# Two blocks of wo per layer, loaded as five columns by sixteen DMA engines and a sixth by six

## The chip, the core and the metric

The kernel runs on one core of one Trainium2 chip. The metric is the device time of one execution in microseconds (us), the median over runs; lower is better. "The profile" is a record of one execution by the hardware profiler, "the trace" the events behind it. Engines: PE does matmuls (PEld its weight loads), DVE and ACT work on vectors, POOL sets constants, SP issues every load; sixteen DMA engines carry the bytes from HBM to SBUF.

## What is computed

One token passes two layers, each an attention over the last 4096 cached keys (32 heads of 192) and a mixer:

```python
q = (x @ wq) in 32 heads of 192
scores = einsum(q, k) * Dh**-0.5          # k, v: the last 4096 of 32768 rows of the caches
o = einsum(softmax(scores), v)            # 32 x 192, as one row of 6144
A(x) = o @ wo                             # wo: 6144 x 640
x = x + A(layernorm(x));  x = x + B(layernorm(x), w1, w2, w3, w4)
x = x + A(layernorm(x));  x = x + B(layernorm(x), w1, w2, w3, w4)
```

With one token every shift in B moves its row out of range, so B is x plus a gelu between w3 and w4. Both layers use the same weights and caches, and nearly all of them are read twice: 216.47 MB from HBM.

## The kernel before

**Groups.** The 32 heads are worked in 8 groups of 4 (QH), backwards in layer 0 and forwards in layer 1. For a head, DVE transposes its keys in 32x32 blocks (line 377), PE forms scores (453), the group's softmax follows (lines 476 to 538), PE multiplies the probabilities with the values (569), and o_fold (578) leaves the group's output in oT: 128 partitions by 6 columns, partition 32 h + r holding elements 6 r to 6 r + 5 of head h. A group's projection by wo waits in `pending` until the next group's first scores are under way.

**Projection.** wo's 768 rows of one group lie in a cell as 128 partitions by 6 columns of 640: partition p holds the rows 6 p to 6 p + 5. In the groups of `rows` (line 726) out_row (608) takes oT's columns one by one as weights and streams wo's columns past them, in two halves of 320, into rows 0 and 32 of a PSUM tile; add (619) adds both rows into `acc` on DVE, and turn_row (629) turns the sum into a column at the end. The other groups use out_proj (591).

**Loads.** All loads are issued on SP in the order of layer_stream (205): wq and x, then K and V loads by turns, with one wo after the four V of a group. A K or V head is 128 partitions of 12288 bytes, 1.5 MB; a wo block 128 of 7680 bytes. They go into 11 cells of SBUF that are taken and given back in turn. The order of each engine's instructions is written out by hand in attention (641); the framework adds the waits. It gives the loads eight completion counters in turn, so that a load also waits until the load eight before it, which used the same counter, has completed.

**Others that the change touches.** `ones` (264), a 128x128 matrix of ones, is the weight of every sum over partitions (lines 325, 338, 528, 681, 866, 868). At the start PE runs 66 small matmuls (WARM, lines 77 and 310) while it waits for loads. row_space (352) gives the room for acc.

Of the kernel before, what the change touches and what calls it, by code (L numbers as in the profile page):

```python
# [8 lines left out]
BF16 = mybir.dt.bfloat16  # L9
F32 = mybir.dt.float32  # L10
# [7 lines left out]
P = 128  # L18
# [17 lines left out]
def kernel(  # L36
# [14 lines left out]
    nc = tc.nc  # L51
    _, _, D = A_x.shape
    _, H, Sk, Dh = A_k_cache.shape
# [20 lines left out]
    NA = Dh // 32  # L74
    NKX = 6
    NKEEP, NCELL = 7, 11
    WARM = 66

# [6 lines left out]
    assert W4C % 2 == 1 and W4C < NF  # L85
    GROUPS = [[list(range(h, h + QH)) for h in range(0, H, QH)] for _ in range(2)]
    GROUPS[0].reverse()

    head = ctx.enter_context(tc.tile_pool(name="head", bufs=1))
    fixed = ctx.enter_context(tc.tile_pool(name="fixed", bufs=1))  # L90
# [66 lines left out]
    def load_wq(layer, kc):  # L157
        nc.sync.dma_start(wq_sb[:, kc, :], A_wq[kc * P:(kc + 1) * P, :])
        return wq_sb

    def load_wo(layer, c):
        t = take(("wo", layer, c))
        src = A_wo[c * QC:(c + 1) * QC, :].rearrange("(p c) n -> p (c n)", c=NA)
        parts = {NG - 2: (3, 3), NG - 1: (3, 2, 1)}.get(c, (NA,)) if layer == 1 else (NA,)
        i = 0
        for n in parts:
            nc.sync.dma_start(t[:, i * D:(i + n) * D], src[:, i * D:(i + n) * D])
            i += n
        return t
# [121 lines left out]

    Lq = const.tile([P, 32], F32, name="Lq")
    nc.vector.reduce_sum(Lq[:], ident[:].rearrange("p (j a) -> p a j", j=4), axis=AX.X)
    eps1 = head.tile([P, 1], F32, name="eps1")
    nc.vector.memset(eps1[:], eps)

# [25 lines left out]
    def ln_center(x, rowsum):  # L322

        mean_ps = psm.tile([P, 1], F32, tag="psm")
        nc.tensor.matmul(mean_ps[:], lhsT=ones[:], rhs=rowsum[:, 0:1], start=True, stop=True)
        xc = big.tile([P, ND], BF16, name="xc")
        nc.vector.scalar_tensor_tensor(out=xc[:], in0=mean_ps[:, 0:1].broadcast_to([P, ND]), scalar=-1.0 / D,
                                       in1=x[:], op0=ALU.mult, op1=ALU.add)
        xcf = big.tile([P, ND], F32, name="xcf")
        nc.vector.scalar_tensor_tensor(out=xcf[:], in0=mean_ps[:, 0:1].broadcast_to([P, ND]), scalar=-1.0 / D,  # L330
                                       in1=x[:], op0=ALU.mult, op1=ALU.add)
        junk = sm.tile([P, ND], F32, tag="ln_junk")
        ssq = sm.tile([P, 1], F32, tag="ln_ssq")
        nc.scalar.activation(junk[:], xcf[:], ACTF.Square, accum_out=ssq[:, 0:1])

        def total():
            var_ps = psm.tile([P, 1], F32, tag="psm")
            nc.tensor.matmul(var_ps[:], lhsT=ones[:], rhs=ssq[:, 0:1], start=True, stop=True)
            return var_ps

        return xc, xcf, total
# [131 lines left out]
    def softmax_steps(n, ST_ps, sc):  # L473
# [25 lines left out]
        def spread_max():  # L499
            nb_ps = psm.tile([P, 1], F32, tag="psm")  # L500
            nc.tensor.matmul(nb_ps[:], lhsT=held["w"],  # L501
                             rhs=ones[0:1, 0:1], start=True, stop=True)
# [14 lines left out]
        def swap():  # L517
            ng = NGK // NT
            PT_ps = psm.tile([P, n, NJ4, NGK], F32, tag="psm")
            src = held["PrT"].rearrange("p (g j i) -> p i j g", g=ng, j=NJ4)  # L520
            for m in range(NM):
                for q in range(NT):
                    nc.tensor.matmul(PT_ps[32 * m:32 * (m + 1), :, :, ng * q:ng * (q + 1)], lhsT=Eq[:, q, :],  # L523
                                     rhs=src[:, m:QW:NM], start=True, stop=True)
            PT = big.tile([P, n, NJ4 * NGK], BF16, name="PT")
            nc.scalar.copy(PT[:].rearrange("p h c -> p (h c)"), PT_ps[:].rearrange("p h j g -> p (h j g)"))  # L526
            l_ps = psm.tile([P, QH], F32, tag="psm")
            nc.tensor.matmul(l_ps[:], lhsT=ones[:], rhs=held["lh"][:], start=True, stop=True)  # L528
            held["lps"] = l_ps
            return PT  # L530

# [73 lines left out]
                give(("wo", layer, c))  # L605
        return y_ps

    def out_row(layer, c, oT, acc, first):

        wo_t = need("wo", layer, c)  # L610
        N = D // 2
        yr_ps = psm.tile([33, N], F32, tag="psm")
        for k in range(NA):
            for i in range(2):
                nc.tensor.matmul(yr_ps[32 * i:32 * i + 1, :], lhsT=oT[:, k:k + 1],  # L615
                                 rhs=wo_t[:, k * D + i * N:k * D + (i + 1) * N], start=(k == 0), stop=(k == NA - 1))
        give(("wo", layer, c))

        def add():
            for i in range(2):  # L620
                r = slice(32 * i, 32 * i + 1)
                if first:
                    nc.vector.tensor_copy(acc[r, :], yr_ps[r, :])
                else:
                    nc.vector.tensor_add(acc[r, :], acc[r, :], yr_ps[r, :])

        return add

    def turn_row(acc):
        y_ps = psm.tile([P, ND], F32, tag="psm")  # L630
        N = D // 2
        for n in range(ND):
            a, b = n * P, (n + 1) * P
            for i in range(2):
                lo_, hi = max(a, i * N), min(b, (i + 1) * N)
                if lo_ < hi:
                    nc.tensor.matmul(y_ps[lo_ - a:hi - a, n:n + 1], lhsT=acc[:, lo_ - i * N:hi - i * N],  # L637
                                     rhs=ident[0:33, 32 * i:32 * i + 1], start=True, stop=True)
        return y_ps

    def attention(layer, x_cur, rs_cur, x_new, z_new, rs_new, ss_new):
# [29 lines left out]
        def add_y(y_ps, n):  # L671
            y_new = x_new if n == 0 else sm.tile([P, ND], F32, name="y_acc")
            if n == 1:

                rs = big.tile([P, 1], F32, name="rs_y")
                nc.vector.scalar_tensor_tensor(out=y_new[:], in0=y_ps[:], scalar=1.0, in1=y[0][:],
                                               op0=ALU.mult, op1=ALU.add, accum_out=rs[:, 0:1])

                def center():
                    nm_ps = psm.tile([P, 1], F32, tag="psm")  # L680
                    nc.tensor.matmul(nm_ps[:], lhsT=ones[:], rhs=rs[:, 0:1], start=True, stop=True)
# [12 lines left out]
            y[0] = y_new  # L694
# [39 lines left out]
        for gi, cur in enumerate(groups):  # L734
            nxt = list(enumerate(groups[gi + 1])) if gi + 1 < len(groups) else []
            ST_n = None
            if nxt:
# [24 lines left out]
                else:  # L762
# [5 lines left out]
                    part_max()  # L768
                    T(h0, 1)
                    S(h0, 0, ST_n, 0)  # L770
                    turn_max()
                    full_max()
                    S(h0, 1, ST_n, 0)
# [6 lines left out]
                        q[0]()  # L780
                    in_row = gi - 1 in rows
                    if pending is not None:
                        y_ps = out_row(layer, *pending, acc, gi - 1 == rows[0]) if in_row else out_proj(layer, pending)
                    turn_p()
                    T(h1, 0)
                    if q:
# [73 lines left out]
    def mixer(layer, x_cur, z, rs_cur, ss_cur, x_new, rs_new):  # L860
# [2 lines left out]


        s1_ps = psm.tile([P, 1], F32, tag="psm")
        nc.tensor.matmul(s1_ps[:], lhsT=ones[:], rhs=rs_cur[:, 0:1], start=True, stop=True)
        s2_ps = psm.tile([P, 1], F32, tag="psm")
        nc.tensor.matmul(s2_ps[:], lhsT=ones[:], rhs=ss_cur[:, 0:1], start=True, stop=True)
# [119 lines left out]
```

## Time and profile before

| | |
|---|---|
| median of 3 runs | 519.93 us (519.73 to 520.03) |
| the profiled execution | 519.84 us |
| its span, first to last instruction | 518.0 us |
| busy: PE, PE weight loads, DVE, ACT | 324.8, 192.6, 295.2, 49.5 us |
| instructions | 9589, of them PE 4146 matmuls and 4146 weight loads |
| moved by DMA | 217.08 MB, 419 GB/s on average |
| mean granted PE clock | 0.700 |

How to read the lines below: a row of "busy tenths" or GB/s cuts the span into 40 equal slices. A window's row gives start and end, its length, the busy time of PE, PEld, DVE, ACT and POOL with the number of instructions, PE's granted clock, the share of the sixteen DMA engines that was busy (packets overlap a little, so it can pass 1) and GB/s. A timeline row gives start, duration, engine, line, operation and tile; SPq is SP's queue of loads. A row of one tile gives the shortest, median and longest duration in ns, the first and the last start in us and the shapes.

### The profile page before, as it was taken

How to read it: one execution, taken by the hardware profiler on the slowest of the kernel's cores; microseconds unless marked ns; L12 is line 12 of the kernel's file. 1: busy time of each engine (PE TensorE's matmuls, PEld its weight loads, DVE VectorE, ACT ScalarE, POOL GpSimd, SP SyncE). 2: the span in 40 equal slices, each digit the busy share in tenths (PEclk: the TensorE clock that was granted, in tenths of full speed). 3: DMA queues.
4: the chain of work that ended last, by engine and by line, in shares of the span. 5: the costliest groups of instructions: out<-in, count | busy, mean ns of one | idle time of the engine just before them, and what ended most of it. 6: DMA issues, size and time to landing. Idle time of an engine off the chain costs nothing.

```text
span 518.0 us, 9589 instructions
## 1 busy us (share of the span) xinstructions
PE 324.8 (63%) x4146; PEld 192.6 (37%) x4146; DVE 295.2 (57%) x589; ACT 49.5 (10%) x175; POOL 4.0 (1%) x16
## 2 busy tenths in 40 slices
PE   2057656666664566767755866777566856648665
PEld 2024334333332334434333634434333433425334
DVE  2067667575584655656624356567675765664722
ACT  1000101010010100001011111001010101001011
POOL 2000000000000000000000000000000000000000
PEclk9999878565586755677665778557785676776855
DMA  8999999999999999999999999999999999999995
GB/s 347 433 425 426 433 426 427 432 428 425 433 426 427 431 426 429 428 426 431 424 425 396 385 426 429 428 428 428 429 426 427 432 428 426 426 434 426 427 416 235
DMA packets 23949, 217.08 MB, mean 419 GB/s; under 512 B 2532, under 2 KB 3044, under 8 KB 8420
## 3 DMA queue, kind: packets, MB, share of 16 engines
q1 hardware_dynamic: 23908, 216.48, 99.0%
q8 instruction: 32, 0.52, 0.4%
q14 instruction: 9, 0.07, 0.0%
HBM read 216.47 MB, written 0.00 MB: 418 GB/s over the span
## 4 chain that ended last, share of the span: by engine, by line
DMA 50%; PE 23%; DVE 22%; issue 2%; ACT 1%; SPq 1%; DVEq 0%; ACTq 0%
DMA cell<-in_A_k_cache_dram 39%; DVE cell L377 16%; DMA cell<-in_A_v_cache_dram 9%; PE ST_ps L453 9%; PE O_ps L569 7%; DVE o_sb L576 2%; DMA cell<-in_B_w_dram 2%; DVE pm L478 1%; PE nb_ps L501 1%; DVE o_sb L512 1%; ACT o_sb L507 1%; PE y_ps L637 1%; PE l_ps L528 1%; PE PT_ps L523 1%; PE qT_ps L407 1%
## 5 line engine op out<-in xcount | busy, mean ns | idle before, releaser
L453 PE MATMUL ST_ps<-cell,Qblk 128*16 128x256 bf16 x1536 | 163.7, 380 | 106.9 <-DVE cell L377 69.4
L377 DVE STREAM_TRANSPOSE cell<-cell 128x768 uint32<-128x768 uint32 x228 | 204.1, 945 | 15.2 <-DMA cell<-in_A_k_cache_dram 14.9
L453 PEld LDWEIGHTS <-Qblk 128*16 128x16 bf16 x1536 | 86.1, 111 | 176.5 <-issue 150.3
L569 PE MATMUL O_ps<-cell,PT 128*2 128x384 bf16 x1018 | 99.9, 461 | 8.2 <-DMA cell<-in_A_v_cache_dram 7.4
L576 DVE STREAM_TRANSPOSE o_sb<-O_ps 128x384 f32<-128x384 f32 x64 | 37.2, 581 | 111.8 <-PE O_ps L569 111.6
L569 PEld LDWEIGHTS <-PT 128*2 128x2 bf16 x1024 | 46.0, 100 | 22.1 <-issue 10.1
L512 DVE STREAM_TRANSPOSE o_sb<-o_sb 128x256 bf16<-128x256 bf16 x16 | 7.1, 446 | 33.2 <-ACT o_sb L507 24.2
L584 ACT ACTIVATE oT<-oT_ps,rl 32x6 bf16<-32x6 f32 x40 | 10.3, 258 | 164.0 <-PE oT_ps L583 157.8
L583 PEld LDWEIGHTS oT_ps<-o_sb,Lq 128*32 128x32 f32 x160 | 13.3, 145 | 19.3 <-issue 15.8
L583 PE MATMUL oT_ps<-o_sb,Lq 128*32 128x6 f32 x160 | 13.9, 195 | 10.4 <-DVE o_sb L576 9.9
L589 ACT ACTIVATE oT<-oT_ps,rl 32x6 bf16<-32x6 f32 x24 | 6.2, 258 | 107.6 <-PE ST_ps L453 87.1
L407 PE MATMUL qT_ps<-xc,wq_sb 128*128 128x1 bf16 x210 | 7.1, 165 | 12.8 <-DMA wq_sb<-in_A_wq_dram 12.0
L523 PE MATMUL PT_ps<-o_sb,Eq 128*32 128x32 bf16 x256 | 7.3, 237 | 9.3 <-DVE o_sb L512 4.1
L523 PEld LDWEIGHTS <-Eq 128*32 128x32 bf16 x256 | 5.4, 108 | 19.8 <-issue 19.7
L421 DVE TENSOR_TENSOR Xq<-qT_ps,maskq 128x24 bf16<-128x24 f32 (+1 forms) x18 | 2.8, 158 | 17.1 <-PE qT_ps L407 17.1
L396 PE MATMUL qr_ps<-wq_sb,xc 128*1 128x384 bf16 x90 | 12.1, 415 | 0.0
L407 PEld LDWEIGHTS <-wq_sb 128*128 128x128 bf16 x210 | 6.7, 102 | 14.0 <-DMA wq_sb<-in_A_wq_dram 13.0
L504 ACT COPY nb_sb<-nb_ps 128x1 f32<-128x1 f32 x16 | 2.5, 159 | 94.6 <-PE nb_ps L501 94.6
L615 PE MATMUL yr_ps<-cell,oT 128*1 128x320 bf16 x108 | 11.2, 355 | 0.0
L528 PE MATMUL l_ps<-lh,ones 128*128 128x4 f32 x32 | 7.7, 310 | 4.9 <-ACT PT L526 4.9
L428 PE MATMUL Qrep_ps<-Xq,Lb 128*128 128x24 bf16 (+1 forms) x18 | 3.2, 178 | 11.1 <-DVE Xq L421 10.8
L588 PE MATMUL oT_ps<-o,Lq 128*32 128x6 f32 x48 | 6.1, 199 | 6.5 <-DVE o L587 6.5
(143 smaller groups left out, 200.9 us busy)
## 6 DMA issues: line engine op xcount, KB each, us to landing
cell<-in_A_k_cache_dram SPq DMA_DIRECT2D x57, 1536.0 KB, 26.3
cell<-in_A_v_cache_dram SPq DMA_DIRECT2D x57, 1536.0 KB, 25.8
cell<-in_A_wo_dram SPq DMA_DIRECT2D x13, 960.0 KB, 26.5
wq_sb<-in_A_wq_dram SPq DMA_DIRECT2D x5, 1536.0 KB, 12.2
cell<-in_A_v_cache_dram SPq DMA_DIRECT2D x4, 768.0 KB, 23.8
cell<-in_A_v_cache_dram SPq DMA_DIRECT2D x2, 1248.0 KB, 11.5
cell<-in_B_w_dram SPq DMA_DIRECT2D x1, 1536.0 KB, 11.9
cell<-in_B_w_dram SPq DMA_DIRECT2D x2, 768.0 KB, 10.3
```

The source lines that it names most:

```text
L377: nc.vector.transpose(Tu, Ku[:, :, q * NY:(q + 1) * NY])
L396: nc.tensor.matmul(qr_ps[32 * i:32 * i + 1, :], lhsT=xc[:, kc:kc + 1], rhs=wq_sb[:, kc, t0 * P + i * N:t0 * P + (i + 1) * N], start=(kc == ...
L407: nc.tensor.matmul(qT_ps[:, tl:tl + 1], lhsT=wq_sb[:, kc, t * P:(t + 1) * P], rhs=xc[:, kc:kc + 1], start=(kc == 0), stop=(kc == ND - 1))
L453: nc.tensor.matmul(ST_ps[r:r + QW, :].rearrange("p (g i) -> p g i", g=ng), lhsT=Q[:, n, :], rhs=T4[:, :, f, :, t], start=(hq == 0 and n == ...
L512: nc.vector.transpose(held["PrT"], held["Pr"])
L523: nc.tensor.matmul(PT_ps[32 * m:32 * (m + 1), :, :, ng * q:ng * (q + 1)], lhsT=Eq[:, q, :], rhs=src[:, m:QW:NM], start=True, stop=True)
L528: nc.tensor.matmul(l_ps[:], lhsT=ones[:], rhs=held["lh"][:], start=True, stop=True)
L569: nc.tensor.matmul(O_ps[r:r + 2, :], lhsT=PT[:, hq, 2 * i:2 * i + 2], rhs=v_pair(V, h, 2 * i * Dh, 2 * Dh), start=(i < 4), stop=(i >= NB - 4))
L576: nc.vector.transpose(o_sb[:], O_ps.rearrange("p (e a c) -> p e c a", e=2, c=NA))
L583: nc.tensor.matmul(oT_ps[r, :], lhsT=Lq[:], rhs=o_sb[:, e, :, e], start=(e == 0), stop=(e == 1))
L584: nc.scalar.activation(oT[r, :], oT_ps[r, :], ACTF.Copy, scale=rl[r, 0:1])
L615: nc.tensor.matmul(yr_ps[32 * i:32 * i + 1, :], lhsT=oT[:, k:k + 1], rhs=wo_t[:, k * D + i * N:k * D + (i + 1) * N], start=(k == 0), stop= ...
```

## The change

Two of the eight wo blocks of each layer (the groups 2 and 3 in the order of work, counted from 0) are loaded in seven loads in place of one. Columns 0 to 4 of all 128 partitions come in one load, packets of 6400 bytes. The sixth column's 128 pieces of 640 elements come in six small loads with packets of 1280 bytes, to 56 partitions and three places behind the five columns. The first four take 24 pieces each, and their source is ordered with an outermost size of six; the fifth takes 24 from three blocks of eight; the sixth takes 8.

So that the pieces meet the right elements of oT, spread_low multiplies oT's sixth column by three constant selections (Sel) into a tile of 64 by 3, which ACT copies to oX. out_row then makes, for these groups, 5 x 2 matmuls with oT and 6 x 2 with oX in place of 6 x 2, into four PSUM rows in place of two, and add works on four rows. acc grows from 33 to 97 partitions, and turn_row's constant (E2) sums the rows in pairs.

`ones` becomes one column, read 128 times by its address pattern. WARM falls from 66 to 14.

```diff
-    WARM = 66
+    WARM = 14
...
+    SPLIT = [{GROUPS[layer][g][0] // QH for g in gs} for layer, gs in enumerate(((2, 3), (2, 3)))]
+    NE, NU, LOW = 6, NA - 1, 24
...
+    def load_wo_split(t, src):
+
+        def low(at, col, rows):
+            nc.sync.dma_start(t[at:at + LOW, col * D:(col + 1) * D],
+                              src[rows:rows + LOW, NU * D:].rearrange("(b a) n -> a b n", a=NE))
+
+        nc.sync.dma_start(t[:, 0:NU * D], src[:, 0:NU * D])
+        for h in range(QH):
+            low(32 * (h % 2), NU + h // 2, 32 * h)
+        rest = src[:, NU * D:].rearrange("(h r) n -> h r n", r=32)[:, LOW:, :]
+        e = slice((NU + 2) * D, (NU + 3) * D)
+        nc.sync.dma_start(t[0:LOW, e], rest[0:QH - 1])
+        nc.sync.dma_start(t[32:64 - LOW, e], rest[QH - 1])
...
     def load_wo(layer, c):
         t = take(("wo", layer, c))
         src = A_wo[c * QC:(c + 1) * QC, :].rearrange("(p c) n -> p (c n)", c=NA)
+        if c in SPLIT[layer]:
+            load_wo_split(t, src)
+            return t
...
-    ones = const.tile([P, P], F32, name="ones")
-    nc.vector.memset(ones[:], 1.0)
+    one = const.tile([P, 1], F32, name="one")
+    nc.vector.memset(one[:], 1.0)
+    ones = one[:, 0:1].broadcast_to([P, P])
...
+    Sel = const.tile([P, 3, P // 2], BF16, name="Sel")
+    nc.gpsimd.memset(Sel[:], 0.0)
...
+    E2 = const.tile([P, 2], F32, name="E2")
+    e4 = ident[:].rearrange("p (s i r) -> p s i r", s=2, i=2)
+    nc.vector.tensor_add(E2[:], e4[:, 0, :, 0], e4[:, 1, :, 0])
...
-        return t[0:33, i:i + D].bitcast(F32), t[0:33, i + D:i + D + QC // 2]
+        return t[0:97, i:i + D].bitcast(F32), t[0:33, i + D:i + D + QC // 2]
...
+    def spread_low(oT):
+
+        oX_ps = psm.tile([P // 2, 3], F32, tag="psm")
+        for j in range(3):
+            nc.tensor.matmul(oX_ps[:, j:j + 1], lhsT=Sel[:, j], rhs=oT[:, NU:NA], start=True, stop=True)
+        oX = big.tile([P // 2, 3], BF16, name="oX")
+        nc.scalar.copy(oX[:], oX_ps[:])
+        return oX
+
...
+        steps = [(0, oT[:, k:k + 1], wo_t[:, k * D:(k + 1) * D]) for k in range(NA if oX is None else NU)]
+        if oX is not None:
+            low = slice(0, LOW), slice(32, 32 + LOW)
+            for j, rs in enumerate((low, low, (low[0], slice(32, 64 - LOW)))):
+                steps += [(2 * r.start, oX[r, j:j + 1], wo_t[r, (NU + j) * D:(NU + j + 1) * D]) for r in rs]
...
-            for i in range(2):
+            for i in range(2 if oX is None else 4):
...
                     S(h0, 0, ST_n, 0)
+                    oX = None
+                    if pending is not None and pending[0] in SPLIT[layer]:
+                        oX = spread_low(pending[1])
                     turn_max()
```

More of the change, by code (lines that the diff above doesn't have):

```diff
@@ L293 @@
     nc.vector.reduce_sum(Lq[:], ident[:].rearrange("p (j a) -> p a j", j=4), axis=AX.X)
+    Sel = const.tile([P, 3, P // 2], BF16, name="Sel")
+    nc.gpsimd.memset(Sel[:], 0.0)
+    i4 = ident[:].rearrange("p (h r) -> p h r", r=32)
+    nc.vector.tensor_copy(
+        Sel[:, 0:2].rearrange("p s (h r) -> p (s h) r", r=32)[:, :, 0:LOW].rearrange("p h (a b) -> p h a b", a=NE),
+        i4[:, :, 0:LOW].rearrange("p h (b a) -> p h a b", a=NE))
+    nc.vector.tensor_copy(Sel[:, 2, 0:LOW].rearrange("p (h r) -> p h r", h=QH - 1), i4[:, 0:QH - 1, LOW:])
+    nc.vector.tensor_copy(Sel[:, 2, 32:64 - LOW], i4[:, QH - 1, LOW:])
+    E2 = const.tile([P, 2], F32, name="E2")
+    e4 = ident[:].rearrange("p (s i r) -> p s i r", s=2, i=2)
+    nc.vector.tensor_add(E2[:], e4[:, 0, :, 0], e4[:, 1, :, 0])
     eps1 = head.tile([P, 1], F32, name="eps1")
@@ L324, in ln_center @@
         mean_ps = psm.tile([P, 1], F32, tag="psm")
-        nc.tensor.matmul(mean_ps[:], lhsT=ones[:], rhs=rowsum[:, 0:1], start=True, stop=True)
+        nc.tensor.matmul(mean_ps[:], lhsT=ones, rhs=rowsum[:, 0:1], start=True, stop=True)
         xc = big.tile([P, ND], BF16, name="xc")
@@ L337, in total @@
             var_ps = psm.tile([P, 1], F32, tag="psm")
-            nc.tensor.matmul(var_ps[:], lhsT=ones[:], rhs=ssq[:, 0:1], start=True, stop=True)
+            nc.tensor.matmul(var_ps[:], lhsT=ones, rhs=ssq[:, 0:1], start=True, stop=True)
             return var_ps
@@ L501, in spread_max @@
             nc.tensor.matmul(nb_ps[:], lhsT=held["w"],
-                             rhs=ones[0:1, 0:1], start=True, stop=True)
+                             rhs=one[0:1, 0:1], start=True, stop=True)
             nb_sb = big.tile([P, 1], F32, name="nb_sb")
@@ L527, in swap @@
             l_ps = psm.tile([P, QH], F32, tag="psm")
-            nc.tensor.matmul(l_ps[:], lhsT=ones[:], rhs=held["lh"][:], start=True, stop=True)
+            nc.tensor.matmul(l_ps[:], lhsT=ones, rhs=held["lh"][:], start=True, stop=True)
             held["lps"] = l_ps
@@ L606, in out_proj, with out_row @@
         return y_ps
-    def out_row(layer, c, oT, acc, first):
+    def spread_low(oT):
[5 more added lines that the diff above has]
+        return oX
+    def out_row(layer, c, oT, acc, first, oX=None):
         wo_t = need("wo", layer, c)
         N = D // 2
-        yr_ps = psm.tile([33, N], F32, tag="psm")
-        for k in range(NA):
+        yr_ps = psm.tile([33 if oX is None else 97, N], F32, tag="psm")
+        steps = [(0, oT[:, k:k + 1], wo_t[:, k * D:(k + 1) * D]) for k in range(NA if oX is None else NU)]
[3 more added lines that the diff above has]
+                steps += [(2 * r.start, oX[r, j:j + 1], wo_t[r, (NU + j) * D:(NU + j + 1) * D]) for r in rs]
+        at = [r for r, _, _ in steps]
+        for k, (r, o, w) in enumerate(steps):
             for i in range(2):
-                nc.tensor.matmul(yr_ps[32 * i:32 * i + 1, :], lhsT=oT[:, k:k + 1],
-                                 rhs=wo_t[:, k * D + i * N:k * D + (i + 1) * N], start=(k == 0), stop=(k == NA - 1))
+                nc.tensor.matmul(yr_ps[r + 32 * i:r + 32 * i + 1, :], lhsT=o, rhs=w[:, i * N:(i + 1) * N],
+                                 start=r not in at[:k], stop=r not in at[k + 1:])
         give(("wo", layer, c))
         def add():
-            for i in range(2):
+            for i in range(2 if oX is None else 4):
                 r = slice(32 * i, 32 * i + 1)
-                if first:
+                if first and i < 2:
                     nc.vector.tensor_copy(acc[r, :], yr_ps[r, :])
@@ L637, in turn_row @@
                     nc.tensor.matmul(y_ps[lo_ - a:hi - a, n:n + 1], lhsT=acc[:, lo_ - i * N:hi - i * N],
-                                     rhs=ident[0:33, 32 * i:32 * i + 1], start=True, stop=True)
+                                     rhs=E2[0:97, i:i + 1], start=True, stop=True)
         return y_ps
@@ L680, in center @@
                     nm_ps = psm.tile([P, 1], F32, tag="psm")
-                    nc.tensor.matmul(nm_ps[:], lhsT=ones[:], rhs=rs[:, 0:1], start=True, stop=True)
+                    nc.tensor.matmul(nm_ps[:], lhsT=ones, rhs=rs[:, 0:1], start=True, stop=True)
                     ym = big.tile([P, ND], F32, name="y_m")
@@ L782, in attention @@
                     if pending is not None:
-                        y_ps = out_row(layer, *pending, acc, gi - 1 == rows[0]) if in_row else out_proj(layer, pending)
+                        y_ps = out_row(layer, *pending, acc, gi - 1 == rows[0], oX) if in_row else out_proj(layer, pending)
                     turn_p()
@@ L865, in mixer @@
         s1_ps = psm.tile([P, 1], F32, tag="psm")
-        nc.tensor.matmul(s1_ps[:], lhsT=ones[:], rhs=rs_cur[:, 0:1], start=True, stop=True)
+        nc.tensor.matmul(s1_ps[:], lhsT=ones, rhs=rs_cur[:, 0:1], start=True, stop=True)
         s2_ps = psm.tile([P, 1], F32, tag="psm")
-        nc.tensor.matmul(s2_ps[:], lhsT=ones[:], rhs=ss_cur[:, 0:1], start=True, stop=True)
+        nc.tensor.matmul(s2_ps[:], lhsT=ones, rhs=ss_cur[:, 0:1], start=True, stop=True)
         def centred(dt, name):
```

## The prediction

> **What bounds the kernel now.** I read the page's DMA rows first, then the queues, then SP's waits and timeline.
>
> ```profile
> DMA  8999999999999999999999999999999999999995
> GB/s 347 433 425 426 433 426 427 432 428 425 433 426 427 431 426 429 428 426 431 424 425 396 385 426 429 428 428 428 429 426 427 432 428 426 426 434 426 427 416 235
> ...
> q1 hardware_dynamic: 23908, 216.48, 99.0%
> q8 instruction: 32, 0.52, 0.4%
> ```
>
> The sixteen DMA engines are busy from end to end, so the stream of loads is the bound. It loses time at two dips only: the layer boundary (396 and 385 GB/s) and the tail (235). The second queue fetches instructions: 32 pieces of 16 KB. What the tail looks like, by windows (the last two columns are DMA share and GB/s):
>
> ```profile
> 510.00:511.00 1.00, 0.21 (x8) 0.12 (x5) 0.00 (x0) 0.00 (x0) 0.00 (x0) 0.50 1.00 397
> 511.00:512.00 1.00, 0.80 (x24) 0.72 (x24) 0.02 (x1) 0.27 (x1) 0.00 (x0) 0.50 0.78 305
> 512.00:513.00 1.00, 0.00 (x0) 0.10 (x1) 0.83 (x7) 0.45 (x2) 0.00 (x0) 0.50 0.53 202
> 513.00:514.00 1.00, 0.73 (x23) 0.67 (x23) 0.83 (x6) 0.69 (x3) 0.00 (x0) 0.50 0.24 90
> ```
>
> The engines do not finish together: half are done 2 us before the last. The trace's completion events (one per engine and load) give the spread: 0.6 us for the load that completes at 25.2 us, 2.1 at 61, 3.6 at 180, 3.3 at 283; 1.0 after the boundary's dry spell (290.2), 3.7 at the end. Each step comes from one fetch: a 16 KB piece takes 0.93 us, the data packet caught behind it 0.96 instead of 0.46, so one engine falls **1.43 us** back. Following each engine's back-to-back packets, I find the first eight fetches on eight different engines, and the ninth (174.1 us) on the first one's again. None of the five engines that carry x's five packets is among the eight. So eight engines take two fetches per layer (2.9 us) and eight take none; the slow eight set the end of each layer.
>
> How loads are issued (start, duration, SP's queue, line):
>
> ```profile
> 14.26 0.33 SPq L145 DMA_DIRECT2D cell<-in_A_v_cache_dram  x1
> 17.96 0.33 SPq L132 DMA_DIRECT2D cell<-in_A_k_cache_dram  x1
> 21.61 0.33 SPq L145 DMA_DIRECT2D cell<-in_A_v_cache_dram  x1
> 25.24 0.33 SPq L132 DMA_DIRECT2D cell<-in_A_k_cache_dram  x1
> ...
> 100.84 0.33 SPq L145 DMA_DIRECT2D cell<-in_A_v_cache_dram  x1
> 104.48 0.33 SPq L167 DMA_DIRECT2D cell<-in_A_wo_dram  x1
> 108.36 0.33 SPq L132 DMA_DIRECT2D cell<-in_A_k_cache_dram  x1
> ```
>
> The first four start within 0.1 us of the full completions, on all sixteen engines, at 14.2, 17.9, 21.6 and 25.2, each of the load eight earlier. A load waits for the eighth before it, so seven are queued ahead: a whole K or V load lasts 3.65 us, and issue to completion is 26.3 us.
>
> **The change, part by part.** All in the profiled execution, 519.84 us (span 518.0 and 1.84 around it; the median of the runs is 519.93).
>
> *Bytes moved between engines.* A 12288-byte packet takes 460 ns, a 7680-byte one 291, so a byte costs 0.0367 ns and 1280 bytes less save 47 ns. Each of 16 engines carries 8 packets of wo: 0.38 us saved per split load, 0.75 per layer, **1.50 us** in all on the eight slow engines if they get none of the sixth column. The new pieces are 1280-byte packets; those of w4's single blocks took 55 ns. Four loads of 24 rows on six engines give 16 packets to each, 24 rows from a source of three blocks 8 more to three of them, 8 rows one more to eight: 25 x 55 = 1.38 us on three engines, 17 x 55 = 0.94 on three, per split. Net of the 0.38 saved: +1.0 and +0.56 per split, +2.0 and +1.1 per layer, inside the light engines' slack of up to 2.7 (3.3 less the 0.6 of the start). I take these six for light ones, like x's five; were they slow ones, it would cost +2.0 per layer instead.
>
> [...]
>
> *The queue.* Each split load is now seven, so the K load after it has the V load ahead of wo as its eighth predecessor. It can't be issued before that V has landed on the **slowest** engine, when only the shortened wo (8 x 244 ns = 1.95 us) and the small ones are left. Completion comes 0.37 us after the last data packet, the issue 0.03 later, and then the data must start. For that last step, the nearest row:
>
> ```profile
> 283.69 3.39 SPq L145 DMA_DIRECT2D cell<-in_A_v_cache_dram  x2
> ```
>
> At 283.69 most light engines had run dry; their first packets ended at 285.61 to 286.10, that is data as if from 1.46 to 1.95 us after the issue. In a second place (issue 264.56) the engines furthest ahead lost 0.17 and 0.27 us, which is 1.45 and 1.63. After 291.01 some packets took 1.9 us, as if from 2.3 to 3.2. The lower end is 0.95, where the first packet's record starts. I take 1.7, in the middle of the nearest row. The slowest engine then idles 0.37 + 0.03 + 1.7 - 1.95 = 0.15 us per split, **0.6 us** for four (0 at 1.45; 1.6 at 1.95).
>
> *The lead is lost.* All engines that are ahead idle until that K arrives: after each split all sixteen start level. Before, one engine's fetch at 138.7 cost nothing, since it hit an engine 1.4 us ahead of those already hit. Now the layer's end is the sum over stretches of the worst engine in each. Split loads were issued at 104.48, 136.03, 342.77 and 371.13; the V ahead of each completes at 130.0, 161.6, 360.2 and 391.8. Fetches start in layer 0 at 25.8 to 118.1 (six), 138.7 and 151.5, 174.1 to 270.8 (seven); in layer 1 at 293.1 to 351.3 (six), 363.7 and 381.5, 394.5 to 502.0 (seven): each of the three stretches has one per engine hit. Three hits per layer in place of two: +1.43 per layer, **+2.86 us**. If data starts at 0.95, a lead of 0.6 survives each split, which spares the engine hit in the middle stretch 0.6: 2.86 - 1.2 = 1.66.
>
> *Compute.* Per split PE gains ten matmuls of L615's kind (0.30 to 0.355 us) and three selections (0.16 each, as L417's); ACT one copy (0.16, L504), DVE two more adds:
>
> ```profile
> L615 PE MATMUL yr_ps<-cell,oT x108: 299/299/474, 81.6 to 469.4; 128*1 128x320 bf16 x108
> L625 DVE TENSOR_TENSOR wx_sb<-wx_sb,yr_ps x8: 454/468/481, 113.6 to 210.2; 1x320 f32<-1x320 f32 x8
> ```
>
> 3.55 + 0.48 + 0.16 + 0.94 = 5.1 us at most. Behind the selections on PE stand the maximum's transpose and the second half's scores; behind the copy on ACT the exponent's bias; behind the adds on DVE a K transpose. They delay cells by up to 5 us, and SP issues 10 to 22 us before an engine needs it there: nothing. Without that cover it would be 20 us. oT is ready a group earlier, and wo lands some 10 us before L615 reads it (132.3 against 142.8), so no new wait there.
>
> *Start-up.* 52 fewer warm-up matmuls end PE's 1.94 us at 4.28 earlier; it then waits for x (7.25) and for wq (21.63) anyway. A slower clock could at most double the 0.85 us of projections after 21.63, under SP's lead of over 20 us: nothing. Sel, E2 and the smaller ones are a few operations of 0.2 us before x arrives, on DVE's idle second. PE loses 104 instructions and gains 104 (weight loads counted), so I keep the count of fetches at 32; those before the first split only come later, within their stretch.
>
> **Sum:** -1.50 + 0.6 + 2.86 = **+1.96**, so 521.8. At data from 1.45: -1.5 + 0 + 2.8 = +1.3 (521.1); at 1.95: -1.5 + 1.6 + 2.86 = +3.0 (522.8).
>
> **Rivals.** *The relief pays* (0.13): the stretches do not add up, because the leads survive; then -1.5, 518.3. For it: the tail's picture. Against: the eight-load wait. *Half and half* (0.15): data starts near 0.95, -1.5 + 1.66 = +0.2, 520.0, within 0.2%. *Deeper holes* (0.12): data starts 2.4 or more after the issue, as after 291.01: -1.5 + 4 x 0.85 + 2.86 = +4.8, 524.6; decisive from 2.0 on. *The wrong engines*: if the six carry fetches, 2 x 2.0 + 0.6 + 2.86 = +7.5, 527.3 (0.03). The split not happening is excluded: the changed program's load list has the 24 small loads.
>
> **How the numbers follow.** The forecast has 0.57. Range 519.0 to 524.0: it cuts off most of the relief's 0.13 and about half of the deep cases. A measurement of this kernel can tell about 0.2%, 1.04 us, from no change. Faster 0.14 (the relief), same 0.15, slower 0.71 (forecast, holes, wrong engines).
>
> **What would show it.** After each split the next K is issued within 0.1 us of the completion of the V ahead of wo; the DMA share dips at about 131, 164, 362 and 395 us; the spread of completions falls from 2 us to under 0.7 after each; each layer shows three fetch steps on its slowest path. The forecast is wrong if the spread stays at 2 us or more through the splits, or if dips of over 1 us on the slowest engine appear.

## The result and the profile after

| | before | after |
|---|---|---|
| median of 5 runs | 519.93 us (519.73 to 520.27) | 526.21 us (525.47 to 527.75) |
| ratio | | 1.0123 (95%: 1.0106 to 1.0141) |
| the profiled execution, its span | 519.84, 518.0 us | 527.75, 526.0 us |

The change costs 6.3 us by the medians and 7.9 us in the two profiled executions, where +1.96 was forecast; the range ended at 524.0. The profiled execution of the changed kernel is the slowest of its five, so what is read from its trace below adds up to some 1.6 us more than the medians differ by.

The page of the changed kernel, DMA rows and queues:

```profile
DMA  8999999999999999999999999998999999999996
GB/s 342 430 429 429 426 431 426 432 428 403 400 429 379 426 428 430 431 420 430 429 426 379 369 428 428 425 430 352 424 429 374 429 427 430 427 430 427 430 414 253
...
q1 hardware_dynamic: 24560, 216.48, 98.1%
q8 instruction: 32, 0.52, 0.4%
```

The bytes and the 32 fetches are as before. Four dips are new (403 and 400, 379, 352, 374), one at each split; the tail has become better (253 in place of 235). The row of busy tenths shows only one of them, as an 8: a slice is 13 us long. Windows of 2 us show more; here are rows at the first, the third and the fourth split (DMA share and GB/s last):

```profile
129.00:131.00 2.00, 1.31 (x13) 0.65 (x12) 2.00 (x3) 0.00 (x0) 0.00 (x0) 0.74 0.85 346
131.00:133.00 2.00, 1.62 (x25) 1.25 (x26) 0.38 (x2) 0.10 (x1) 0.00 (x0) 0.50 0.67 218
133.00:135.00 2.00, 1.01 (x14) 0.45 (x6) 0.75 (x2) 0.16 (x1) 0.00 (x0) 0.91 0.96 393
...
365.00:367.00 2.00, 1.51 (x21) 0.72 (x19) 1.53 (x3) 0.00 (x0) 0.00 (x0) 0.62 0.44 117
367.00:369.00 2.00, 2.00 (x27) 1.22 (x24) 0.00 (x0) 0.26 (x1) 0.00 (x0) 0.53 0.79 313
...
399.00:401.00 2.00, 1.16 (x17) 0.65 (x7) 0.81 (x2) 0.26 (x1) 0.00 (x0) 0.85 0.81 202
```

The last row has a second loss beside the idling: the engines are busy for 0.81 of the window and move only 202 GB/s. The kernel before in the second and the third of these windows:

```profile
131.00:133.00 2.00, 1.72 (x25) 1.30 (x26) 0.28 (x2) 0.20 (x1) 0.00 (x0) 0.50 1.03 441
133.00:135.00 2.00, 1.03 (x12) 0.31 (x5) 0.75 (x2) 0.06 (x1) 0.00 (x0) 0.50 0.95 406
```

PE's and DVE's columns are alike in both kernels (131 to 133: PE 1.62 us after and 1.72 before, DVE 0.38 and 0.28), so the compute is not what stalled. SP's timeline at the first split:

```profile
102.92 0.33 SPq L147 DMA_DIRECT2D cell<-in_A_v_cache_dram  x1
105.69 0.33 SPq L169 DMA_DIRECT2D cell<-in_A_wo_dram  x1
108.46 11.88 SPq L166 DMA_DIRECT2D cell<-in_A_wo_dram  x4
123.25 0.74 SPq L174 DMA_DIRECT2D cell<-in_A_wo_dram  x1
126.89 0.30 SPq L175 DMA_DIRECT2D cell<-in_A_wo_dram  x1
130.58 0.35 SPq L134 DMA_DIRECT2D cell<-in_A_k_cache_dram  x1
132.48 0.33 SPq L147 DMA_DIRECT2D cell<-in_A_v_cache_dram  x1
132.90 0.46 SPq L134 DMA_DIRECT2D cell<-in_A_k_cache_dram  x1
```

Seven of the eight counters went to one wo block (a row with x4 or x2 stands for that many loads). The next K is issued 24.9 us after wo (130.58 after 105.69), where before it was 3.9 (108.36 after 104.48), and 0.06 us after the V ahead of wo has landed on all engines (130.52); then a burst follows as wo and the small loads complete.

**Where the time went.** The bytes are the same, so an engine's time differs almost only by idling and by packets that take longer than the usual time of their size (460 ns for 12288 bytes, 291 for 7680, 244 for 6400, 55 for 1280). Summed from the trace's packets and divided by sixteen (us per engine, up to the last weight packet):

| | idle before | idle after | longer packets before | after |
|---|---|---|---|---|
| around the four splits | 0.10 | 5.22 | 0.08 | 1.95 |
| layer boundary (280 to about 301) | 1.09 | 1.57 | 1.06 | 1.55 |
| tail (last 7 to 9 us) | 1.93 | 1.09 | 0.00 | 0.03 |
| all the rest | 1.58 | 1.50 | 1.70 | 2.13 |

That is +7.50 of the 7.63 by which the last packet ends later; 7.0 of it lies around the splits. The relief moves bytes from some engines to others, so in an average over engines it can only show in the tail: 0.84 us less idling there.

**Theories.** Holes: the queue of loads runs short at each split, since the next K is issued so late (idle engines, and then long first packets). Rivals: small loads on few engines cost by themselves; the added compute or the start-up; moving bytes to engines that are late.

### The profile page after: what moved, and what is told of

Its sections match the earlier page's. It is cut to its first block, busy times and chain, and to the rows that moved or that the text cites. A ratio compares the mean times of both kernels' runs of the same rounds, so it can differ in the third digit from the quotient of the medians.

```text
span 526.0 us, 9630 instructions
## 1 busy us (share of the span) xinstructions
PE 325.3 (62%) x4146; PEld 191.2 (36%) x4146; DVE 299.2 (57%) x601; ACT 50.1 (10%) x179; POOL 4.2 (1%) x17
## 4 chain that ended last, share of the span: by engine, by line
DMA 36%; PE 32%; DVE 27%; issue 3%; ACT 1%; SPq 1%; DVEq 0%; ACTq 0%
DMA cell<-in_A_k_cache_dram 22%; DVE cell L408 19%; DMA cell<-in_A_v_cache_dram 12%; PE ST_ps L484 11%; PE O_ps L600 10%; DVE o_sb L607 3%; DMA cell<-in_B_w_dram 2%; PE qr_ps L427 1%; PE l_ps L559 1%; PE yr_ps L661 1%; PE PT_ps L554 1%; PE nb_ps L532 1%; DVE wx_sb L671 1%; PE y_ps L683 1%; DVE pm L509 1%
## 5 line engine op out<-in xcount | busy, mean ns | idle before, releaser
L484 PE MATMUL ST_ps<-cell,Qblk 128*16 128x256 bf16 x1536 | 159.1, 370 | 109.9 <-DVE cell L408 69.8
L484 PEld LDWEIGHTS <-Qblk 128*16 128x16 bf16 x1536 | 83.1, 109 | 180.1 <-issue 154.3
L600 PE MATMUL O_ps<-cell,PT 128*2 128x384 bf16 x1018 | 102.3, 472 | 9.3 <-DMA cell<-in_A_v_cache_dram 8.6
L559 PE MATMUL l_ps<-lh,one 128*128 128x4 f32 x32 | 8.0, 322 | 5.0 <-ACT PT L557 5.0
L532 PEld LDWEIGHTS nb_ps<-one,o_sb 1*128 1x128 f32 x32 | 6.8, 264 | 7.2 <-issue 5.3
```

The costliest lines, as they stand in the source:

```text
L484: nc.tensor.matmul(ST_ps[r:r + QW, :].rearrange("p (g i) -> p g i", g=ng), lhsT=Q[:, n, :], rhs=T4[:, :, f, :, t], start=(hq == 0 and n == ...
L532: nc.tensor.matmul(nb_ps[:], lhsT=held["w"], rhs=one[0:1, 0:1], start=True, stop=True)
L559: nc.tensor.matmul(l_ps[:], lhsT=ones, rhs=held["lh"][:], start=True, stop=True)
L600: nc.tensor.matmul(O_ps[r:r + 2, :], lhsT=PT[:, hq, 2 * i:2 * i + 2], rhs=v_pair(V, h, 2 * i * Dh, 2 * Dh), start=(i < 4), stop=(i >= NB - 4))
```

## The experiments

Times are medians, with the ratio to the kernel before, run beside them (519.86 us for e1 to e4, 520.05 for e5 to e8, 519.89 for e9 to e11, 520.38 for e12 to e14), and its 95% interval. "Split idle" and "split extra" (from packets that take longer) are the two terms of the table above, summed over the four splits. The edits are shown in part; "..." stands for what is left out.

### e1: four small loads in place of six

```diff
-    NE, NU, LOW = 6, NA - 1, 24
+    NE, NU, LOW, CUT = 6, NA - 1, 48, 1
...
-        for h in range(QH):
-            low(32 * (h % 2), NU + h // 2, 32 * h)
...
+        low(NU, 0, LOW, NE)
+        low(NU + 1, LOW, LOW, NE)
+        low(NU + 2, 2 * LOW, 24, 3)
+        nc.sync.dma_start(t[32:40, (NU + 2) * D:(NU + 3) * D], src[120:128, NU * D:])
```

> The changed kernel with the sixth column in four small loads per split in place of six: 48, 48, 24 and 8 pieces, the same packets on the same engines (16 on each of six, 8 more on three, one more on eight), with the selections rebuilt to match and 8 matmuls with oX in place of 12. A split is five loads in place of seven, so the K load after it waits for the V load two places further back, with a K, a V and wo still queued (about 9 us). Theory of the holes: none of the four holes is left and the engines keep their leads through the splits, so only the relief remains: 519.93 - 1.5 = 518.4 us (517.5 to 519.5). Rival, small packets or few engines cost the time: 526. Rival, the added compute or the start-up: 525.5 to 526.

523.53 us, 1.0073 (1.006 to 1.0087): between all expectations. The holes are gone (split idle 0.10), but split extra is 2.49: for some 2.5 us at each split packets on all engines take 1.2 to 1.4 times as long while none idles.

```profile
129.00:131.00 2.00, 1.72 (x16) 0.90 (x17) 1.68 (x3) 0.00 (x0) 0.00 (x0) 0.50 1.01 396
131.00:133.00 2.00, 2.00 (x29) 1.31 (x23) 0.00 (x0) 0.26 (x1) 0.00 (x0) 0.50 1.05 336
133.00:135.00 2.00, 0.64 (x5) 0.18 (x3) 0.75 (x2) 0.26 (x1) 0.00 (x0) 0.50 1.00 424
```

Share 1.05 at 336 GB/s: a full queue that moves less. So the edit brought in something that e12, with the changed kernel's own small loads, shows next to nothing of (split extra 0.41).

### e2: the same, cut back to seven loads

```diff
-    NE, NU, LOW, CUT = 6, NA - 1, 48, 1
+    NE, NU, LOW, CUT = 6, NA - 1, 48, 2
```

The two loads of 48 pieces are cut in two by columns, in packets of 640 bytes.

> The kernel of e1_four_loads with its two loads of 48 pieces each cut in two by columns, so that a split is seven loads again; nothing else differs (packets of 640 bytes in place of 1280 in these loads). Theory of the holes: the holes are back, 1.4 to 2.4 us three times and 0.8 once, and the leads are lost again: 526 us (524 to 528). Rival, small packets: at most 2 us above e1. Rival, the compute: equal to e1.

525.64 us, 1.0109 (1.0095 to 1.0123), 2.1 us above e1. The dips are back, as expected, but e1 was no clean base, and 2.1 us is barely more than the 2 that small packets were given.

### e3: the compute without the loads

```diff
-        if c in SPLIT[layer]:
-            load_wo_split(t, src)
-            return t
...
-                steps += [(2 * r.start, oX[r, j:j + 1], wo_t[r, (NU + j) * D:(NU + j + 1) * D]) for r in rs]
+                steps += [(2 * r.start, oX[r, j:j + 1], wo_t[r, NU * D:NA * D]) for r in rs]
```

> The changed kernel with all wo blocks loaded in one load as before; selections, the 22 matmuls, four rows, the one column of ones, 14 warm-up matmuls and the larger acc stay. The matmuls with oX read the sixth column in place of the columns behind it, so the output differs from the reference's. Theory of the holes: 519.9 us (519.3 to 520.5). Rival, the added compute or the start-up carries the loss: 526.

519.74 us, 0.9998 (0.9987 to 1.0009). Selections, 22 matmuls, four rows, one column of ones and 14 warm-up matmuls cost nothing. That rival falls.

### e4: seven loads on sixteen engines, nothing else

```diff
+            nc.sync.dma_start(t[:, 0:e], src[:, 0:e])
+            for a, b in ((0, 16), (16, 32), (32, 48), (48, 64), (64, 96), (96, 128)):
+                nc.sync.dma_start(t[a:b, e:NA * D], src[a:b, e:])
```

> The kernel before, with the same two wo blocks per layer in seven loads: columns 0 to 4 of all partitions, and the sixth column in six loads of 16, 16, 16, 16, 32 and 32 partitions, which sixteen engines share evenly; no other change, and nothing is moved between engines. Theory of the holes: 0.44 us per split more is left in the queue (eight 1280-byte packets of 55 ns on each engine), so holes of 6.7 - 4 x 0.44 = 5.0 us, the lost leads 2.9, no relief: 527.8 us (525 to 529). Rivals of few engines and of compute: 519.9 (519.5 to 520.5).

524.80 us, 1.0097 (1.0083 to 1.011), just under the range. Split idle 2.70, extra 2.30: most of the loss comes without few engines and without added compute. (These loads cover 16 or 32 partitions; e14 repeats the step with loads of all 128.)

### e5 and e6: five and nine such loads

```diff
-            for a, b in ((0, 16), (16, 32), (32, 48), (48, 64), (64, 96), (96, 128)):
+            for a, b in [(q, q + 32) for q in range(0, P, 32)]:
```

This is e5; e6 takes steps of 16.

> The kernel of e4_seven_on_sixteen with the sixth column in four loads of 32 partitions in place of six, so five loads per split: the same bytes on the same engines, and a K, a V and wo still queued when the next K is issued. Holes as the cause of e4's 4.9 us: 519.9 us (519.3 to 520.6), no dip at the splits, spread of completions kept at 2 us and more. Rival, small packets slow their neighbours wherever they run (0.6 us per split as in e1): 522.3. Rival, splitting costs as such: 524.8.

523.43 us (522.07 to 528.69 in 12 runs), 1.007 (1.0049 to 1.0092), not the 519.3 to 520.6 of the holes. No idle engines (0.16), as that theory has it, but split extra 2.40, as in e1, now on sixteen engines: few engines are not what slows the packets.

> The same with the sixth column in eight loads of 16 partitions, nine loads per split: the next K now waits for the first of the small loads, so behind the wait nothing of wo is left to hide it. From V's last completion to K's last took 6.4 us in e4 three times; with wo's 1.95 us no longer beside the wait 8.4. Holes: 4 x 2.0 = 8 us over e4, 532.8 us (531 to 534.5). Rival, a cost per small load: 2 x 4 loads more than e4, 524.8 + 4.9 x 8 / 24 = 526.4.

534.67 us, 1.0278 (1.0262 to 1.0294), just above the holes' range and far from the rival's 526.4. Split idle 13.36: the K now waits for the first small load, behind wo's five columns, and the stream stops.

```profile
129.00:131.00 2.00, 0.62 (x8) 0.37 (x9) 2.00 (x3) 0.00 (x0) 0.00 (x0) 1.00 0.75 300
131.00:133.00 2.00, 1.51 (x20) 0.68 (x15) 1.38 (x3) 0.00 (x0) 0.00 (x0) 0.55 0.17 59
133.00:135.00 2.00, 1.91 (x25) 1.14 (x21) 0.05 (x1) 0.26 (x1) 0.00 (x0) 0.60 0.66 147
```

### e7 and e8: nearer pieces; four engines

```diff
-                                  src[rows:rows + h, NU * D + i:NU * D + i + w].rearrange("(b a) n -> a b n", a=a))
+                                  near[rows:rows + h, i:i + w].rearrange("(b a) n -> a b n", a=a))
```

This is e7 against e1, with `near` a view of the block's rows of 640; e8 against e1:

```diff
-    NE, NU, LOW, CUT = 6, NA - 1, 48, 1
+    NE, NU, LOW, CUT = 4, NA - 1, 48, 1
...
-        low(NU + 2, 2 * LOW, 24, 3)
+        low(NU + 2, 2 * LOW, 24, 4)
```

and the load of 8 pieces by four as well.

> The kernel of e1_four_loads, but the three larger small loads read 1280-byte pieces that lie next to each other in wo (rows of the same block, in place of every sixth row of 640), so the output differs from the reference's; packets, engines and partitions are the same. If the slowing of all engines by a third beside the small packets (0.6 us per split in e1) comes from the distance between the pieces that are read: 523.5 - 2.4 = 521.1 us. If not: 523.5 (522.7 to 524.3).

524.87 us (524.05 to 527.72), 1.010 (1.0075 to 1.0124), above both expectations: the slowing is still there (split extra 2.4), so the distance between the pieces in HBM is not its cause. What makes e7 slower than e1 is not known; its trace has one more slow stretch, told with e12.

> The kernel of e1_four_loads, but every small load is ordered with an outermost size of four, so that four engines carry all 128 pieces of the sixth column, 32 each. In e1's completions four of the six engines end the first small load 0.7 us after the first wo completion, the other two 2.2 and 2.6 after it: two of the six are engines that have been hit by fetches. If these two carry part of e1's loss and the four are the lowest-numbered ones: from V to K the slowest engine gains 0.38 and loses the 0.6 of the slowing per split, 4 x 0.2 = +0.9, 520.8 us (520.0 to 522.0). If bytes on late engines do not matter: 523.5; if the lightest four are not among them: 525 or more.

525.55 us, 1.011 (1.0091 to 1.0129), as expected if a late engine is among the four. At the first split the four engines complete the first small load 0.81, 0.96, 0.96 and 2.11 us after wo's first completion; at the second 2.28, 2.43, 2.47 and 4.61, where wo's own last was 4.02. One of these four is a late engine. The prediction had taken all six for light ones. No trace numbers the engines, so whether these four are the lowest-numbered ones is not shown.

### e9 and e10: two loads; five by rows

```diff
-            for a, b in [(q, q + 32) for q in range(0, P, 32)]:
+            for a, b in ((0, P),):
```

That was e9; e10:

```diff
+            for a, b in ((0, 64), (64, 80), (80, 96), (96, 112), (112, P)):
+                nc.sync.dma_start(t[a:b, 0:NA * D], src[a:b, :])
```

> The kernel of e5_five_on_sixteen with the sixth column of all 128 partitions in one load in place of four: a split is two loads, the same packets on the same sixteen engines. In e5 every packet took 1.2 to 1.5 times as long for 2.5 us per split. If the number of loads brings that: 519.9 us (519.3 to 520.6). If 1280-byte packets beside K packets bring it, however they are issued: 522.3 to 523.4, as e5.

520.92 us, 1.0015 (1.0005 to 1.0025), 0.3 us above its range and well under e5's; split idle 0.14, extra 0.08. The 128 packets of 1280 bytes slow nothing at the splits. Where the 1.0 us by the medians goes is not shown.

> The kernel before with the same two wo blocks per layer in five loads by partitions, 64, 16, 16, 16 and 16 of them, each with whole 7680-byte packets: as many loads as e5, no small packets, the same bytes on the same engines. If the number of loads brings the slowing: 522.3 to 523.4 us, as e5. If the small packets bring it: 519.9 (519.3 to 520.6).

535.95 us (534.02 to 538.93), 1.0306 (1.0283 to 1.033): far outside both. No small packets, as many loads as e5, no idle engine (0.06), and a split extra of 14.8 us:

```profile
127.00:129.00 2.00, 0.28 (x1) 0.09 (x1) 2.00 (x3) 0.00 (x0) 0.00 (x0) 1.00 1.11 364
129.00:131.00 2.00, 1.23 (x12) 0.56 (x12) 2.00 (x4) 0.00 (x0) 0.00 (x0) 0.71 0.88 192
131.00:133.00 2.00, 1.98 (x27) 1.68 (x28) 0.01 (x1) 0.26 (x1) 0.00 (x0) 0.50 1.08 267
```

By the packets themselves the slowing is 1.9 to 2.0 in the first part (128.5 to 131.0), where the load of 64 partitions comes first, and 1.65 to 1.9 after. So neither packet size nor number: what e1, e5, e7, e8 and e10 share is that their loads cover some of the partitions only.

### e11: three loads

```diff
-    NE, NU, LOW = 6, NA - 1, 24
+    NE, NU, LOW, CUT = 6, NA - 1, 120, 1
...
+        low(NU, 0, LOW, NE)
+        nc.sync.dma_start(t[LOW:P, NU * D:NA * D], src[LOW:P, NU * D:])
```

> The changed kernel with the sixth column in two small loads, 120 pieces on six engines (20 each) and 8 pieces on eight, so three loads per split; one selection and 2 matmuls with oX. Two of the six engines are late ones: they gain 0.38 us and lose 20 x 0.055 = 1.1 per split, +0.72. If the slowing comes with the number of loads and is gone here: 4 x 0.72 = +2.9, 522.8 us. If it comes with small packets: 4 x (0.72 + 0.6) = +5.3, 525.2. If late engines do not matter and no slowing is left: 518.4.

525.23 us, 1.0101 (1.0083 to 1.012). It meets the number for small packets, but after e9 and e10 not their reason: e9's 128 packets of 1280 bytes had a split extra of 0.08. What in the load of 120 pieces costs the time is not shown.

### e12: the changed kernel with its loads spread

```diff
+        for item in seq:
+            out.append(item)
+            if parts:
+                out.append(parts.popleft())
+            if item[0] == "wo" and item[2] in SPLIT[layer]:
+                parts += [("wos",) + item[1:] + (i,) for i in range(3)]
+                out.append(parts.popleft())
```

> The changed kernel with nothing but the order of its loads changed: after the five columns come two of the small loads, then the next K, two more, the next V, and the last two. The same 24 small loads with the same packets, engines and partitions, the same compute; but the K after a split now waits for a load seven places ahead, and at least two whole K or V loads (7.3 us) stay queued. In the changed kernel's trace the sixteen engines idled 1.3 us each at each of the four splits and their packets took 0.5 us longer, 7.0 us in all. Theory of the holes: all of that is gone. What is left is the relief of the late engines without small pieces, and two late engines of the six which gain 0.38 and lose 0.94 per split, so the last engine ends up to 2.2 us later than before: 520.5 us (518.4 to 522). Rival, small loads on few engines cost by themselves: 524 to 526.

524.14 us, 1.0062 (1.0041 to 1.0083), in two groups: 521.3 to 521.5 in four of ten runs, 524.1 to 525.4 in six. The median misses the 518.4 to 522 of the holes and lies in the rival's 524 to 526; only the lower group lies where the holes put it. At the splits themselves the holes are gone. SP's timeline and the windows:

```profile
104.87 0.33 SPq L187 DMA_DIRECT2D cell<-in_A_wo_dram  x1
108.09 4.37 SPq L171 DMA_DIRECT2D cell<-in_A_wo_dram  x2
115.50 0.34 SPq L134 DMA_DIRECT2D cell<-in_A_k_cache_dram  x1
119.09 4.35 SPq L171 DMA_DIRECT2D cell<-in_A_wo_dram  x2
126.44 0.34 SPq L147 DMA_DIRECT2D cell<-in_A_v_cache_dram  x1
```

```profile
129.00:131.00 2.00, 1.34 (x13) 0.56 (x12) 2.00 (x3) 0.00 (x0) 0.00 (x0) 0.82 1.02 424
131.00:133.00 2.00, 1.58 (x25) 1.21 (x26) 0.41 (x2) 0.07 (x1) 0.00 (x0) 0.50 1.11 471
```

The K is issued 15 us earlier than in the changed kernel; split idle is 0.22 and extra 0.41 in place of 5.22 and 1.95. Counted from V's last completion, wo completes 0.36 to 0.38 us earlier at each split, the relief to the digit. Two of the six engines are late: at the first split their first small load ends 1.20 and 1.68 us after wo's first completion, those of the other four 0.21 to 0.29. That these two give the relief back in the next loads is an argument: the spread of K's completions after the last three splits is 3.24, 2.56 and 3.12 us, against 2.00, 2.25 and 2.77 before, and 1.96, 2.35 and 2.42 in e9, which moves nothing between engines.

The profiled execution is one of the upper group (524.17), and its trace has a slow stretch behind the last split:

```profile
402.00:430.00 28.00, 17.40 (x221) 10.06 (x217) 18.74 (x34) 3.21 (x11) 0.00 (x0) 0.79 1.01 390
432.00:437.00 5.00, 2.56 (x35) 1.47 (x33) 2.72 (x5) 0.52 (x2) 0.00 (x0) 0.79 1.01 425
```

From 402 to 432 us packets take 1.11 times as long on all engines, 2.6 us in all; then the rate is back. The groups lie 2.6 to 4.0 us apart, so the stretch may be what parts them, but only one execution was traced. The first slowed packets start at 402.25, as the last two small loads of the fourth split land (402.31 and 402.95). e7's profiled execution has the same stretch, running on from its fourth split to 434; none of the other fourteen traces has one, that of the kernel before among them. So the small loads may set it off, and the rival is not excluded for the upper group. No edit was made to tell the cause; it stays open. The lower group, about 521.4, stands 1.0 us above the median of the kernel before beside it, and 2.0 above that kernel's fastest run (519.38).

### e13 and e14: cut by columns

```diff
-            for a, b in [(q, q + 32) for q in range(0, P, 32)]:
-                nc.sync.dma_start(t[a:b, e:NA * D], src[a:b, e:])
+            for a, n in [(160 * i, 160) for i in range(4)]:
+                nc.sync.dma_start(t[:, e + a:e + a + n], src[:, e + a:e + a + n])
```

This is e13; e14 makes six cuts of 104 and 112, so seven loads per split with the five columns.

> The kernel of e5_five_on_sixteen, five loads per split on sixteen engines, with the sixth column cut by columns (four times 160 of 640 elements, all 128 partitions) in place of partitions (four times 32). [...] If that brings the slowing of e5 (packets 1.2 to 1.5 times as long for 2.5 us per split) and of e10: 519.9 to 520.9 us, as e9. If the number of loads or the size of packets (320 bytes here) brings it: 522.5 to 524.5.

520.92 us, 1.0011 (1.0000 to 1.0022), at the upper end of its range; split idle 0.24, extra 0.07 against e5's 2.40. As many loads as e5, smaller packets, and no slowing: e5's came with the cut by partitions. First e5's window, then e13's:

```profile
131.00:133.00 2.00, 2.00 (x28) 1.31 (x23) 0.00 (x0) 0.26 (x1) 0.00 (x0) 0.50 1.06 366
```

```profile
131.00:133.00 2.00, 2.00 (x27) 1.18 (x22) 0.00 (x0) 0.26 (x1) 0.00 (x0) 0.54 1.02 411
```

Why loads of some of the partitions slow the packets is not shown: the traces do not say which engine writes which partition. Nor do they show why e12's small loads, the largest on 24 partitions, slow next to nothing (split extra 0.41), where e1's, the largest on 48, reach 2.49.

> [...] Theory of the holes: idle time and long first packets at four places as in the changed kernel, less what the small packets cover: 525 us (523.5 to 526.5). If e4's 4.9 us came from partitions alone: 520.9.

525.18 us, 1.0089 (1.0076 to 1.0102), on the expected number. Split idle 2.65, extra 2.20, together 4.85 where the medians differ by 4.80 from the kernel before. e14's windows at the first split:

```profile
129.00:131.00 2.00, 1.51 (x16) 0.69 (x14) 1.42 (x3) 0.00 (x0) 0.00 (x0) 0.58 0.92 331
131.00:133.00 2.00, 2.00 (x27) 1.17 (x21) 0.00 (x0) 0.26 (x1) 0.00 (x0) 0.56 1.03 318
```

From e13 to e14 there are only two more loads per split (and packets of 208 to 224 bytes in place of 320): 4.3 us by the medians. In e13 the next K is issued at 122.79 us, 7.3 us before the V ahead of wo has landed; in e14 at 130.16, 0.06 us after. This is the hole alone.

## Why the prediction was wrong

**Right.** The mechanism and its place: the K after a split is issued 0.06 to 0.07 us after the V ahead of wo completes, the dips stand at 130 to 132.5, 163.5 to 166.5, 363.5 to 367 and 398.5 to 400.5 us. The price of an issue: K's first engine completes as if its data had started 1.36 to 1.52 us after the issue (1.7 taken). Compute and start-up at nothing (e3, 519.74 us against 519.86; the lowest granted clock in the traces of both kernels is 0.50, the highest 1.00), and the fetches still 32. The relief of 0.38 per split as such (e12). A sum without a term for each load as such: e13's sixteen small loads cost 0.5 us by the medians.

**Wrong, the step that carries the miss:** the queue's term, 0.15 us per split (0.6 in all), and with it "after each split all sixteen start level". From V's last completion to K's last took 5.91, 5.92, 5.92 and 6.45 us before and 6.98, 7.83, 7.68 and 6.35 after, +4.6 in all, where relief and hole together should have given -0.9. That is 5.5 us more than predicted, nearly the whole miss in the profiled execution. The prediction counted when the first data come and let all engines go on at their usual rate from there. The first engine did come back on time; the last came 1.36, 2.38, 2.08 and 0.79 us behind it, where the prediction's own sign was a spread of under 0.7. After the dry spell (the time without queued packets) the first packets took up to 1.0 to 1.45 us in place of 0.46 on many engines at once, 0.4 to 0.65 us per engine and split. The row for that was in hand: packets of 1.9 us after 291.01, which the prediction used only to date the start of the data. In the third split a fetch (370.95) hit one engine inside that K as well. Of the rivals, the wrong engines (527.3) came nearest in size and deeper holes (524.6) next, neither for its reason: the first wanted all six engines late, the second wanted the data later, and they were on time.

**Not settled: the lost leads.** What the changed kernel lost outside the stretches from V to K is 3.0 us (7.6 by the last completion, less 4.6), close to the 2.86 put down, but it is a remainder in which other costs can hide. The same remainder is 3.0 in e2 and e6, 1.8 in e4 and 0.15 in e14, whose queues run short in the same way. So the sign, slower, was forecast through a term that the runs do not confirm: that it came true is in part luck.

**Wrong, without effect on the sign:** the six engines are not all light. The prediction took them for light ones like x's five, which no run shows, and two of them are late: in the changed kernel's first split they complete the first small load 1.16 and 1.97 us after wo's first completion, the other four 0.25 to 0.39. For these two the pieces add 0.56 us per split, by the prediction's own prices, in place of saving 0.38 (the load that only three engines share has no late completion, 131.50 to 131.61). The relief did not pay even without the holes: e12 stays 1.0 us above the kernel before in its faster group. How much of that the late engines cost is not shown, since e9 stands 1.0 us above too and moves nothing between engines. The rival "the relief pays" falls with e12, and "the wrong engines" was true for two of six.

**What stays open:** why the first packets after a dry spell are long; the 1.11 stretch of e7 and e12, and whether the small loads set it off; how the 0.8 to 2.4 us divide on single engines, since the trace does not name them; the price of the lost leads. A relief through engines that are light all along was not tried. No version here beats the kernel before.

## What to carry to other kernels

Count loads, not only bytes, where completions are waited for in turn: with eight counters and wo cut into seven loads, the next K was issued 0.06 us after the V ahead of wo had landed, with only wo's loads left in the queue (e14, 525.18 us); with wo cut into five, 7.3 us before (e13, 520.92 us). Pieces put between large loads lost 0.6 us at the splits in place of 7.2 (e12), though that kernel was still slower than the one before. Five loads cut by columns did better here than five cut by partitions (e13 against e5: split extra 0.07 against 2.40, 520.92 us against 523.43). And read first how long the engines wait, on average, at the next place where all must be done: 1.9 us at the tail and 1.1 at the boundary by the table above. That this caps a gain from evening out engines is an estimate from these two numbers that no run tests.

## What the runs showed of the hardware

- A load of 64 partitions and four of 16 behind it made all engines' packets take 1.65 to 2.0 times as long for 7 us (e10); loads of 32, 1.2 to 1.5 times (e5). Loads of all 128, 160 or 640 elements wide, slowed no packets at the splits (extra 0.07 and 0.08 in e13 and e9).
- In e12's full queue the packets of the small loads took 55 ns for 1280 bytes, as in w4's blocks before, and the split extra was 0.41 us over four splits.
- After a dry spell the first engine's data started 1.36 to 1.62 us after the issue, worked back from its completion (sixteen splits of four kernels: the changed one, e2, e4, e6), and the longest of the first 12288-byte packets took 1.0 to 1.45 us in the changed kernel, where the usual one takes 0.46.
